# Attention and experts on one core: resident expert weights, batched gating, slot tables by one-hot matmuls, scatter in place

## The chip, the core and the metric

The kernel runs on one core of a Trainium2 chip. The metric is the device time of one execution in microseconds. PE is the matrix engine, DVE the vector engine, ACT the scalar engine, POOL the GpSimd engine, SP the engine that here only issues DMAs.

## The reference

Attention over 4 batches, 8 heads, 768 positions of 64 elements, then a layer of eight experts over the 3072 rows x of 512 elements that attention gives:

```python
scores = scale * np.matmul(q, k.transpose(0, 1, 3, 2))
# retrieval heads (0, 2, 6): causal; the others: causal and (first 4 or last 64 positions)
a = softmax(where(mask, scores, -1e9)); x = a @ v
do_compute = x @ w_skip > 0                 # other rows: out = x
logits = xc @ w_gate; e_idx = argmax(logits); gate_w = softmax(logits)[e_idx]
for e in range(8):
    h = np.maximum(xc[e_idx == e] @ w1[e], 0.0)
    y[e_idx == e] = gate_w * (h @ w2[e])
out[do_compute] = xc + y
```

w1[e] is 512 x 1024, w2[e] 1024 x 512, all inputs fp32.

## The kernel before

*Attention* (L162 to L277). For each batch b and pair of heads ("head group", hg, 16 in all) POOL issues six loads that cast to fp16: qin and kin for two heads (L172, L174), va for each (L197), 96 KB each. PE transposes q and k (L180, L184). Per head, `qk_exp` (L212) does a matmul of scores pst (L217), ACT the exponential into ats (L223), DVE a mask (L226, L249); then PE accumulates opsa (L268), and DVE divides into xsb, which holds all of x (L276). qin and kin have four buffers, va six. DVE writes the column of ones in va (L199) after its load has landed.

*Gating* (L284 to L327), per block of 128 rows, six per batch: PE transposes the block in fp32 (gxtp, one PSUM buffer, L289), DVE casts it (L293), PE multiplies by the gate and skip weights (L297), and some twelve DVE operations and one exponential on ACT give the gate and a one-hot row over the experts. x also goes to DRAM, attn_x (L280).

*Routing* (L333 to L421), after the last batch: ranks by fp32 matmuls and a running sum over 24 blocks (L351) give each token a slot; each expert has ECAP = 384 slots. 24 scatters on POOL write token numbers to eight tables in DRAM (L404); these are read back (L412), merged (L416), turned (L419).

*Experts* (L441 to L501). POOL issues the two weight loads of an expert (w1t, w2t, casts to fp16, two buffers, L444, L445), then for each of three blocks of 128 slots a gather of rows of attn_x (xg, L456) and one of gates (gw, L463); empty slots are skipped by the bounds check, over a tile set to zero. DVE scales (L468), PE transposes in fp32 (L472), DVE casts (L475). Chunks of 256 and 128 slots: PE multiplies by w1 (hps, L481), ACT takes the relu (L488), PE multiplies by w2 (yps, L493), DVE copies (L498), and the result goes to y_sorted in DRAM.

*End* (L505 to L518). For each of 24 blocks a gather fetches the rows of y_sorted by token (fyg, L510), DVE adds xsb (L516), and SP or ACT stores.

A scheduler fixes the order of each engine's instructions at build time; each engine runs its own in order and waits on semaphores. A POOL DMA also waits for the POOL DMA eight before it.

Of the kernel before, what the change touches and what calls it, by code (L numbers as in the profile page):

```python
# [9 lines left out]
FP32 = mybir.dt.float32  # L10
FP16 = mybir.dt.float16
# [7 lines left out]
B = 4  # L19
# [16 lines left out]
MTOK = 256  # L36
ECAP = MTOK + P


@with_exitstack  # L40
def kernel(
# [14 lines left out]
    nc = tc.nc  # L56

    NSLOT = E * ECAP
    NSUB = ECAP // P
    NC = N // P  # L60
    DS = DM // P
    FS = F // P
    NS2 = (NSLOT + P) // P
    NSHARD = 8
    BIG_IDX = 1 << 16

    X = nc.dram_tensor("attn_x", (N, DM), FP32, kind="Internal").ap()
    GATE = nc.dram_tensor("gate_w", (N,), FP32, kind="Internal").ap()
    SH = [nc.dram_tensor(f"sorted_sh{i}", (NSLOT + P,), I32,
                         kind="Internal").ap() for i in range(NSHARD)]  # L70
    YS = nc.dram_tensor("y_sorted", (NSLOT, DM), FP32, kind="Internal").ap()

    const = ctx.enter_context(tc.tile_pool(name="const", bufs=1))
    persist = ctx.enter_context(tc.tile_pool(name="persist", bufs=1))

    ident = const.tile([P, P], FP16, name="ident")
    make_identity(nc, ident)
# [3 lines left out]
    utri = const.tile([P, P], FP32, name="utri")  # L81
    nc.gpsimd.memset(utri, 1.0)
    nc.gpsimd.affine_select(
        out=utri, in_=utri, compare_op=ALU.is_ge, fill=0.0,
        base=0, pattern=[[1, P]], channel_multiplier=-1)

    ones_col = const.tile([P, 1], FP32, name="ones_col")
    nc.gpsimd.memset(ones_col, 1.0)
    ones_row = const.tile([1, P], FP32, name="ones_row")
    nc.gpsimd.memset(ones_row, 1.0)  # L90
    e_row8 = const.tile([P, E], FP32, name="e_row8")
    erow8i = const.tile([P, E], I32, name="erow8i")
    nc.gpsimd.iota(erow8i, pattern=[[1, E]], base=0, channel_multiplier=0)
    nc.vector.tensor_copy(e_row8, erow8i)

    bigfill = const.tile([NS2, P], I32, name="bigfill")
    nc.vector.memset(bigfill, BIG_IDX)
    for i in range(NSHARD):
        (nc.sync if i % 2 else nc.scalar).dma_start(
            out=SH[i].rearrange("(n p) -> n p", p=P),  # L100
            in_=bigfill)

    xsb = persist.tile([P, B, NQB, H, D], FP32, name="xsb")
# [11 lines left out]
    maskp = ctx.enter_context(tc.tile_pool(name="maskp", bufs=1))

    def band_mask(name, q_off, lo, hi, sink=False, width=P):
        m = maskp.tile([P, width], FP16, name=name)
        nc.gpsimd.memset(m, 1.0)
        nc.gpsimd.affine_select(  # L120
            out=m, in_=m, compare_op=ALU.is_ge, fill=0.0,
            base=q_off - lo, pattern=[[1, width]], channel_multiplier=-1)
        if hi is not None:
            nc.gpsimd.affine_select(
                out=m, in_=m, compare_op=ALU.is_ge, fill=0.0,
                base=hi - q_off, pattern=[[-1, width]], channel_multiplier=1)
        if sink:
            sm = maskp.tile([P, width], FP16, name=name + "_s")
            nc.gpsimd.memset(sm, 1.0)
            nc.gpsimd.affine_select(  # L130
                out=sm, in_=sm, compare_op=ALU.is_ge, fill=0.0,
                base=N_SINK - 1, pattern=[[0, width]], channel_multiplier=-1)
            nc.gpsimd.affine_select(
                out=sm, in_=sm, compare_op=ALU.is_ge, fill=0.0,
                base=q_off, pattern=[[1, width]], channel_multiplier=-1)
            nc.vector.tensor_max(m, m, sm)
        return m

    retr_diag = band_mask("retr_diag", 0, 0, None)
    strm_d0 = band_mask("strm_d0", 0, 0, WINDOW - 1, sink=True)  # L140
    strm_dn = band_mask("strm_dn", 0, 0, WINDOW - 1)
    strm_s0 = band_mask("strm_s0", QB, 0, WINDOW - 1, sink=True)
    strm_sn = band_mask("strm_sn", QB, 0, WINDOW - 1)
# [4 lines left out]
    vv = v.rearrange("b h (n p) d -> b h n p d", p=P)  # L148
    Xv = X.rearrange("(b n p) (h d) -> b n p h d", b=B, p=P, h=H)
# [404 lines left out]
```

## Time and profile before

| what | before |
|---|---|
| median of 3 runs (lowest, highest) | 503.02 us (502.21, 506.92) |
| span of the profiled execution | 499.5 us |
| busy PE / DVE / ACT / POOL | 313.7 / 208.8 / 135.2 / 202.8 us |
| DMA moved in the span | 50.51 MB, 101 GB/s |

The span goes from the first to the last instruction. [...] GB/s count bytes written, so a transfer that casts fp32 to fp16 counts half of what it reads.

### The profile page before, as it was taken

What the parts mean: (1) busy time and instruction counts of PE and PEld (TensorE: products, weight loads), DVE (VectorE), ACT (ScalarE), POOL (GpSimd) and SP (SyncE); (2) the same over time, 40 slices, a digit from 0 to 9 for tenths busy, and PEclk for the clock granted to TensorE, in tenths of its full rate; (3) what the DMA queues carried; (4) which work ended last, traced back from release to release, by engine and by line L of the source; (5) the groups of instructions that cost most, each with busy time, mean ns of one, the idle gap of its engine ahead of it and who ended that gap; (6) DMA issues with size and microseconds to landing.
All of it is one profiled execution on the core that took longest, in us unless ns stands there. A gap on an engine that the chain in (4) does not pass through costs nothing.

```text
span 499.5 us, 6050 instructions
## 1 busy us (share of the span) xinstructions
PE 313.7 (63%) x1981; PEld 175.0 (35%) x1981; DVE 208.8 (42%) x883; ACT 135.2 (27%) x317; POOL 202.8 (41%) x269
## 2 busy tenths in 40 slices
PE   0699999998999999962000048766868668770000
PEld 0344454444444444331000035534535444540000
DVE  1245566455654665467000134141441423316563
ACT  1464646564645564610000002101111012020000
POOL 9976751553011100000674636342533525005662
PEclk9999999999999999999999999979699798896555
DMA  4999991999132511031000694959679589512675
GB/s 31 120 103 88 82 202 11 70 65 173 11 25 18 142 10 8 2 126 2 1 0 9 112 206 112 170 126 206 122 162 168 122 162 183 125 52 95 211 229 184
DMA packets 108207, 50.51 MB, mean 101 GB/s; under 512 B 85079, under 2 KB 93671, under 8 KB 108176
## 3 DMA queue, kind: packets, MB, share of 16 engines
q0 software_dynamic: 94240, 31.04, 54.1%
q10 hardware_dynamic: 6000, 10.59, 6.0%
q1 hardware_dynamic: 7936, 8.51, 5.0%
q8 instruction: 15, 0.25, 0.2%
q14 instruction: 16, 0.13, 0.1%
HBM read 65.14 MB, written 19.00 MB: 168 GB/s over the span
## 4 chain that ended last, share of the span: by engine, by line
PE 45%; DMA 22%; issue 9%; POOL 9%; DVE 7%; ACT 6%; ACTq 0%; POOLq 0%; SPq 0%; DVEq 0%
DMA xg<-attn_x,merged 14%; PE pst L217 13%; PE opsa L268 10%; PE yps L493 6%; PE hps L481 5%; PE gxtp L289 4%; ACT ats L223 3%; ACT ht L488 2%; POOL fyg L510 2%; DMA fyg<-y_sorted,slot_i 2%; DMA gw<-gate_w,merged 2%; POOL sorted_sh L404 2%; PE qTps L180 2%; PE kTps L184 2%; DMA sorted_sh<-row_idx,slot_i 2%
## 5 line engine op out<-in xcount | busy, mean ns | idle before, releaser
L223 ACT ACTIVATE ats<-pst 128x256 f16<-128x256 f32 (+4 forms) x236 | 92.6, 417 | 74.1 <-PE pst L217 71.8
L217 PE MATMUL pst<-qT,kT 64*128 64x256 f16 (+4 forms) x236 | 91.0, 426 | 3.8 <-ACT ats L223 1.0
L488 ACT ACTIVATE ht<-hps 128x2048 f16<-128x2048 f32 (+1 forms) x16 | 23.2, 1450 | 196.8 <-PE hps L481 134.2
L268 PE MATMUL opsa<-va,ats 128*128 128x65 f16 x552 | 69.8, 241 | 2.9 <-ACT ats L223 2.3
L197 POOL DMA_DIRECT2D va<-in_v_dram x32 | 26.7, 843 | 94.0 <-PE opsa L268 54.5
L493 PE MATMUL yps<-w2t,ht 128*128 128x512 f16 x192 | 52.8, 433 | 18.7 <-ACT ht L488 18.7
L268 PEld LDWEIGHTS <-ats 128*128 128x128 f16 x552 | 41.3, 117 | 54.7 <-DVE ats L226 12.2
L481 PE MATMUL hps<-xTm,w1t 128*128 128x128 f16 (+1 forms) x512 | 48.0, 255 | 1.0 <-DVE xTm L475 1.0
L404 POOL DMA_INDIRECT sorted_sh<-row_idx,slot_i x24 | 23.4, 977 | 57.2 <-DVE slot_i L398 50.2
L481 PEld LDWEIGHTS <-w1t 128*128 128x128 f16 x512 | 42.0, 102 | 10.4 <-issue 3.8
L510 POOL DMA_INDIRECT fyg<-y_sorted,slot_i x24 | 26.5, 1104 | 42.2 <-DVE fyg L509 37.7
L472 PE MATMUL xtp<-identf,xg 128*128 128x128 f32 x96 | 18.9, 351 | 36.2 <-DVE xg L468 36.2
L468 DVE TENSOR_SCALAR xg<-xg,gw 128x512 f32<-128x512 f32 x24 | 11.4, 492 | 67.8 <-DMA xg<-attn_x,merged 52.2
L493 PEld LDWEIGHTS <-ht 128*128 128x128 f16 x192 | 19.2, 107 | 47.2 <-ACT ht L488 23.2
L456 POOL DMA_INDIRECT xg<-attn_x,merged x24 | 24.8, 1033 | 22.4 <-issue 19.0
L217 PEld LDWEIGHTS <-kT 64*128 64x128 f16 (+1 forms) x236 | 20.5, 102 | 27.8 <-issue 16.2
L289 PE MATMUL gxtp<-identf,xsb 128*128 128x128 f32 x96 | 29.3, 435 | 0.9 <-DVE xsb L276 0.9
L174 POOL DMA_DIRECT2D kin<-in_k_dram x32 | 27.8, 867 | 3.8 <-PE kTps L184 2.6
L172 POOL DMA_DIRECT2D qin<-in_q_dram x32 | 27.7, 866 | 3.0 <-PE pst L217 2.0
L475 DVE CAST xTm<-xtp 128x512 f16<-128x512 f32 x24 | 15.8, 681 | 30.7 <-PE xtp L472 30.7
L180 PE MATMUL qTps<-ident,qin 128*128 128x128 f16 x96 | 18.8, 308 | 14.9 <-DMA qin<-in_q_dram 14.9
L472 PEld LDWEIGHTS xtp<-identf,xg 128*128 128x128 f32 x96 | 14.7, 181 | 37.8 <-DVE xg L468 20.6
(111 smaller groups left out, 369.1 us busy)
## 6 DMA issues: line engine op xcount, KB each, us to landing
w1t<-in_moe_w_dram POOLq DMA_DIRECT2D x8, 1024.0 KB, 9.4
w2t<-in_moe_w_dram POOLq DMA_DIRECT2D x8, 1024.0 KB, 12.3
y_sorted<-ys ACTq DMA_DIRECT2D x16, 256.0 KB
qin<-in_q_dram POOLq DMA_DIRECT2D x32, 96.0 KB, 3.3
kin<-in_k_dram POOLq DMA_DIRECT2D x32, 96.0 KB, 3.3
va<-in_v_dram POOLq DMA_DIRECT2D x32, 96.0 KB, 3.2
attn_x<-xsb SPq DMA_DIRECT2D x12, 256.0 KB
attn_x<-xsb ACTq DMA_DIRECT2D x12, 256.0 KB
```

The lines of the kernel that those rows point to most:

```text
L174: nc.gpsimd.dma_start(out=kin[:, :, hd, :], in_=kv[b, h0 + hd].transpose([1, 0, 2]))
L180: nc.tensor.matmul(qTps[:, n * P:(n + 1) * P], qin[:, n].rearrange("p h d -> p (h d)"), ident, is_transpose=True, start=(n == 0), stop=(n ...
L217: nc.tensor.matmul(pst[:k_rows, :qn], kTh[:, j * P:j * P + k_rows], qTh[:, q_lo:q_hi], start=True, stop=True)
L223: nc.scalar.activation(dst, pst[:k_rows, :qn], ACT.Exp)
L268: nc.tensor.matmul(opsa[:, i, :], ats[:kr, sl, i * QB:i * QB + QB], vh[:kr, j, :], start=(cnt == 1), stop=(cnt == total))
L289: nc.tensor.matmul(xtp[:, s, :], xc[:, s * P:(s + 1) * P], identf, is_transpose=True, start=(s == 0), stop=(s == DS - 1))
L404: nc.gpsimd.indirect_dma_start(out=SH[c % NSHARD][:, None], out_offset=bass.IndirectOffsetOnAxis(ap=slot_i[:, c:c + 1], axis=0), in_=row_i ...
L472: nc.tensor.matmul(xtp[:, s, :], xg[:, s * P:(s + 1) * P], identf, is_transpose=True, start=(s == 0), stop=(s == DS - 1))
L481: nc.tensor.matmul(hps[:, fs, :mt], w1t[:, s, fs * P:(fs + 1) * P], xT[:, s, :mt], start=(s == 0 and fs % BPB == 0), stop=(s == DS - 1 and ...
L488: nc.scalar.activation(ht[:, :, :mt], hps[:, :, :mt], ACT.Relu)
L493: nc.tensor.matmul(yps, ht[:, fs, s2 * P:(s2 + 1) * P], w2t[:, fs, :], start=(fs == 0), stop=(fs == FS - 1))
L510: nc.gpsimd.indirect_dma_start(out=yg, out_offset=None, in_=YS[:, :], in_offset=bass.IndirectOffsetOnAxis(ap=slot_i[:, c:c + 1], axis=0), ...
```

## The change

Attention keeps its loops. The weights of all experts get places of their own in SBUF (w1a, w2a), and POOL issues the two loads of one expert in every second head group. qin and kin have two buffers, va four, qT and kT two. x of a batch is in one tile xb with one buffer, stored straight to `out` by SP in one DMA per batch. The gating of a batch is done for its six blocks at once (`gate_ops`), and goes on to ranks (a matmul with a lower triangle, one with ones, a scan), and to one-hot tables: Lall (which of 128 slots in a tile) and Rall (which of 16 tiles, times token number and gate). 24 matmuls of Lall with Rall give, for each slot, its token and gate (mps). Each expert has CAP = 256 slots. 16 gathers fetch rows of `out`; an empty slot reads some row, and its scatter index is out of bounds. The gate is applied in the update of the gathered rows, which a scatter then writes back to `out`. PE does the first half of expert e + 1 before the second half of e. At the end every engine reads a flag (an expert with over 256 tokens, or other retrieval heads than 0, 2, 6) and branches past `general_path`, a slow form of the whole program in loops.

```diff
+CAP = 256
+NT = E * CAP // P
...
+    w1a = wpool.tile([P, E, DS, F], FP16, name="w1a")
+    w2a = wpool.tile([P, E, FS, DM], FP16, name="w2a")
...
-    with tc.tile_pool(name="qk_in", bufs=4) as qk_in_pool, \
-         tc.tile_pool(name="qt", bufs=3) as qt_pool, \
-         tc.tile_pool(name="va", bufs=6) as v_pool, \
+    with tc.tile_pool(name="qk_in", bufs=2) as qk_in_pool, \
+         tc.tile_pool(name="qt", bufs=2) as qt_pool, \
+         tc.tile_pool(name="va", bufs=4) as v_pool, \
+         tc.tile_pool(name="xsb", bufs=1) as x_pool, \
...
+                if hg % 2 == 1:
+                    ew = 2 * b + hg // 2
+                    nc.gpsimd.dma_start(out=w1a[:, ew], in_=w1r[ew])
+                    nc.gpsimd.dma_start(out=w2a[:, ew], in_=w2r[ew])
...
+            nc.sync.dma_start(out=Ov[b], in_=xbf)
...
+            gate_ops(nc, gat_pool, C, glog, NQB, gate,
+                     oh.rearrange("p e n -> p n e"))
...
+            nc.tensor.matmul(cps, ones16, ohf, start=True, stop=True)
+            nc.tensor.matmul(rps, lneg, ohf, start=True, stop=True)
...
+            nc.vector.tensor_tensor(
+                Rall[:, b], oht.unsqueeze(3).to_broadcast([P, NQB, NT, 4]),
+                val.unsqueeze(2).to_broadcast([P, NQB, NT, 4]), op=ALU.mult)
+            for n in range(NQB):
+                nc.vector.tensor_scalar(Lall[:, b, n], iota16,
+                                        posf[:, 1, n:n + 1], None,
+                                        ALU.is_equal)
...
+        for c in range(N // P):
+            nc.tensor.matmul(
+                mps.rearrange("p t v -> p (t v)"), Lall[:, c // NQB, c % NQB],
+                Rall[:, c // NQB, c % NQB].rearrange("p t v -> p (t v)"),
+                start=(c == 0), stop=(c == N // P - 1))
...
+        for t in range(NT):
+            xg = xg_pool.tile([P, DM], FP32, name=f"xg{t}")
             nc.gpsimd.indirect_dma_start(
+                out=xg, out_offset=None, in_=out[:, :],
...
+            for f2 in range(FS // 2):
+                hps = h_psum.tile([P, 2, CAP], FP32, tag="hps", name="hps")
...
+                            hps[:, fi, :], w1a[:, e, s, fs * P:(fs + 1) * P],
+                            xT[:, s, :], start=(s == 0), stop=(s == DS - 1))
+                nc.scalar.activation(ht[:, 2 * f2:2 * f2 + 2], hps, ACT.Relu)
...
+                nc.vector.scalar_tensor_tensor(xgs[t], yps, gsl[:, t:t + 1],
+                                               xgs[t], ALU.mult, ALU.add)
                 nc.gpsimd.indirect_dma_start(
+                    out=out[:, :],
...
+        first(0)
+        for e in range(E):
+            if e + 1 < E:
+                first(e + 1)
+            second(e)
+
+    flag = nc.values_load(flagi[:, :])
+    with tc.If(flag > 0, preferred_fallthrough_block=False):
+        general_path(tc, C, q, k, v, moe_w1, moe_w2, out, XG, FL, nz)
```

`first` is casts, transposes and hps with the relu of an expert, `second` its yps, updates and scatters.

On POOL, in the experts of the kernel before, one expert's transfers stand in the queue like this (weights, three gathers of rows, gates):

```order
L444 DMA w1t<-in_moe_w_dram 128x4x1024
L445 DMA w2t<-in_moe_w_dram 128x8x512
L456 DMA xg<-attn_x,merged 128x512 x3
L462 MEMSET gw 128x1
L463 DMA gw<-gate_w,merged 128x1
```

In the kernel after, the weights of the second expert stand on POOL among the loads of the fourth and fifth head groups:

```order
L383 DMA kin<-in_k_dram 128x6x64
L406 DMA va<-in_v_dram 128x6x64
L413 DMA w1a<-in_moe_w_dram 128x4x1024
L406 DMA va<-in_v_dram 128x6x64
L414 DMA w2a<-in_moe_w_dram 128x8x512
L381 DMA qin<-in_q_dram 128x6x64
```

The weights moved from before each expert's gathers to attention, between v loads, each of which waits for a buffer that a head two groups back has read.

On DVE, from the last head of the last batch on, before (xsb is that head's output, then block by block):

```order
L276 TENSOR_TENSOR xsb<-opsa,rec 128x6x64
L293 CAST gxT<-gxtp 128x512
L300 COPY glog<-gp 128x9
L304 MAX mx<-glog 128x8
L318 TENSOR_SCALAR dc<-glog 128x1
L305 MAX_INDEX mi<-mx,glog 128x8
L312 TENSOR_SCALAR neg_mx<-mx 128x1
```

And after, from the same place (xb for xsb; then all six blocks, then one chain):

```order
L490 TENSOR_TENSOR xb<-opsa,rec 128x6x64
L507 CAST gxT<-gxtp 128x512 x6
L513 COPY glog<-gps 128x54
L75 TENSOR_REDUCE g_mx<-glog 128x6
L88 TENSOR_SCALAR g_nd<-glog 128x6
L78 TENSOR_TENSOR g_sub<-glog,g_mx 128x48
L82 SCALAR_TENSOR_TENSOR g_eq<-g_sub,erev 128x48
```

The small operations of each block moved behind the last of the six casts, and are there once instead of six times.

On DVE, from the end of the routing into the experts, before:

```order
L398 CAST slot_i<-slot_f 128x24
L416 TENSOR_REDUCE mnp<-shard_t 25x128
L421 CAST merged<-mnp_ps 128x25
L468 TENSOR_SCALAR xg<-xg,gw 128x512 x2
L475 CAST xTm<-xtp 128x4x128
```

And after (Lall is the last table, msb the slot table copied from PSUM, x_3058 and x_3066 the first two gathered blocks in fp16):

```order
L579 TENSOR_SCALAR Lall<-iota_109,posf 128x128 x5
L593 COPY msb<-mps 128x64
L595 TENSOR_SCALAR emp<-msb 128x16
L597 SCALAR_TENSOR_TENSOR tok<-msb 128x16
L608 TENSOR_TENSOR gsl<-msb 128x16
L601 TENSOR_TENSOR egs<-emp,slot_126 128x16
L599 TENSOR_SCALAR tok<-tok 128x16
L603 TENSOR_TENSOR idx_g<-tok,egs 128x16
L605 SCALAR_TENSOR_TENSOR idx_s<-emp,tok 128x16
L641 CAST x_3058<-xg_2993 128x512
L641 CAST x_3066<-xg_2997 128x512
L647 COPY xT<-xtp 128x4x128
```

Between `slot_i` and `mnp` before lie the scatters and the read-back in DRAM; after, the indices come from PSUM by DVE alone. The next row after these is the third block's cast, and with it the second copy of the transposed block.

## Rows read from the trace of the kernel before

**Rows 1.** Windows by stage: length; busy PE, PEld, DVE, ACT, POOL; PEclk, DMA, GB/s.

```profile
17.00:214.30 197.30, 185.05 (x1113) 91.45 (x1113) 106.94 (x618) 107.04 (x287) 70.75 (x92) 1.00 0.76 69
214.30:227.50 13.20, 6.85 (x45) 4.48 (x45) 10.37 (x74) 2.36 (x12) 0.00 (x0) 1.00 0.33 120
227.50:296.00 68.50, 5.59 (x17) 3.60 (x18) 12.51 (x47) 0.00 (x0) 33.05 (x34) 1.00 0.31 50
296.00:449.20 153.20, 113.86 (x792) 74.18 (x791) 47.88 (x89) 23.20 (x16) 56.13 (x74) 0.88 0.70 144
449.20:499.50 50.30, 0.00 (x0) 0.00 (x0) 28.15 (x49) 0.00 (x0) 26.50 (x24) 0.55 0.56 178
```

**Rows 2.** The chain that ended last: start, length, what.

```profile
260.60 9.65 DMA sorted_sh<-row_idx,slot_i
...
315.60 13.32 DMA xg<-attn_x,merged
...
418.27 11.38 DMA xg<-attn_x,merged
```

**Rows 3.** Timeline of DVE from the last batch's gating into the routing.

```profile
214.88 0.69 DVE L293 CAST gxT<-gxtp 128x512 f16<-128x512 f32 x1 [0.57 <-PE gxtp L289]
...
224.92 0.69 DVE L293 CAST gxT<-gxtp 128x512 f16<-128x512 f32 x1 [0.26 <-PE gxtp L289]
...
225.97 0.17 DVE L300 COPY glog<-gp 128x9 f32<-128x9 f32 x1
...
228.59 0.36 DVE L340 TENSOR_TENSOR rank_in<-incl_ps,onehot 128x192 f32<-128x192 f32 x1 [0.78 <-PE incl_ps L338]
...
229.69 4.28 DVE L351 TENSOR_TENSOR excl<-excl,cnt 1x8 f32<-1x8 f32 x23
```

**Rows 4.** Groups by form, whole span: busy us, mean ns, idle before.

```profile
L223 ACT ACTIVATE ats<-pst 128x512 f16<-128x512 f32 x36 | 21.4, 596 | 8.6 <-PE pst L217 7.5
...
L498 DVE COPY ys<-yps 128x512 f32<-128x512 f32 x24 | 16.5, 685 | 21.0 <-PE yps L493 21.0
...
L468 DVE TENSOR_SCALAR xg<-xg,gw 128x512 f32<-128x512 f32 x24 | 11.4, 492 | 67.8 <-DMA xg<-attn_x,merged 52.2 <-DMA gw<-gate_w,merged 15.4
...
L191 DVE COPY kT<-kTps 128x768 f16<-128x768 f16 x16 | 8.8, 552 | 3.4 <-PE kTps L184 1.9 <-PE pst L217 1.4
...
L325 DVE TENSOR_TENSOR onehot<-e_row,ef 128x8 f32<-128x8 f32 x24 | 3.6, 152 | 0.0
```

**Rows 5.** Timeline of PE in the experts.

```profile
296.08 5.86 PE L481 MATMUL hps<-xTm,w1t 128*128 128x256 f16 x32 [1.01 <-DVE xTm L475]
...
312.18 3.66 PE L481 MATMUL hps<-xTm,w1t 128*128 128x256 f16 x32
315.68 0.60 PE L472 MATMUL xtp<-identf,xg 128*128 128x128 f32 x4
317.87 3.63 PE L493 MATMUL yps<-w2t,ht 128*128 128x512 f16 x16 [1.59 <-ACT ht L488]
321.33 1.95 PE L481 MATMUL hps<-xTm,w1t 128*128 128x128 f16 x32
...
353.44 3.60 PE L493 MATMUL yps<-w2t,ht 128*128 128x512 f16 x8 [0.90 <-ACT ht L488]
```

**Rows 6.** Windows of three shorter stretches, columns as in rows 1.

```profile
280.00:302.00 22.00, 7.86 (x43) 6.21 (x43) 3.80 (x7) 0.02 (x1) 12.01 (x15) 1.00 1.15 204
12.50:25.00 12.50, 8.69 (x58) 4.69 (x58) 2.58 (x12) 5.17 (x11) 12.50 (x16) 1.00 1.89 120
350.00:357.00 7.00, 5.07 (x15) 2.09 (x15) 4.27 (x8) 1.02 (x1) 4.07 (x6) 0.50 0.30 83
```

**Rows 7.** DMA queue of plain stores: packets, MB, share of 16 engines.

```profile
q10 hardware_dynamic: 6000, 10.59, 6.0%
```

**Rows 8.** Timeline of the end: POOL's second gather, the last store's issue.

```profile
454.28 1.00 POOL L510 DMA_INDIRECT fyg<-y_sorted,slot_i  x1 [0.30 <-DVE fyg L509]
...
495.51 0.34 ACTq L517 DMA_DIRECT2D out_dram<-foc  x1
```

**Rows 9.** Tile fyg, gathers at the end with no weights ahead.

```profile
DMA to landing us min/median/max: 2.5/3.6/4.7
```

More of the change, by code (lines that the diff above doesn't have):

```diff
@@ L34, with band_mask @@
 P = 128
-MTOK = 256
-ECAP = MTOK + P
+DS = DM // P
+FS = F // P
+CAP = 256
+NT = E * CAP // P
+BIG_IDX = 1 << 16
+class Consts:
+    pass
+def band_mask(nc, pool, name, q_off, lo, hi, sink=False, width=P):
+    m = pool.tile([P, width], FP16, name=name)
+    nc.gpsimd.memset(m, 1.0)
+    nc.gpsimd.affine_select(
+        out=m, in_=m, compare_op=ALU.is_ge, fill=0.0,
+        base=q_off - lo, pattern=[[1, width]], channel_multiplier=-1)
+    if hi is not None:
+        nc.gpsimd.affine_select(
+            out=m, in_=m, compare_op=ALU.is_ge, fill=0.0,
+            base=hi - q_off, pattern=[[-1, width]], channel_multiplier=1)
+    if sink:
+        sm = pool.tile([P, width], FP16, name=name + "_s")
+        nc.gpsimd.memset(sm, 1.0)
+        nc.gpsimd.affine_select(
+            out=sm, in_=sm, compare_op=ALU.is_ge, fill=0.0,
+            base=N_SINK - 1, pattern=[[0, width]], channel_multiplier=-1)
+        nc.gpsimd.affine_select(
+            out=sm, in_=sm, compare_op=ALU.is_ge, fill=0.0,
+            base=q_off, pattern=[[1, width]], channel_multiplier=-1)
+        nc.vector.tensor_max(m, m, sm)
+    return m
@@ L56 @@
     nc = tc.nc
[L58 to L71, printed above, removed]
+    C = Consts()
@@ L91 @@
[L91 to L103, printed above, removed]
@@ L115 @@
[L115 to L137, printed above, removed]
@@ L139 @@
[L139 to L143, printed above, removed]
+    C.wg = const.tile([P, DS, E + 1], FP16, name="WgAll")
+    nc.gpsimd.dma_start(out=C.wg[:, :, :E],
+                        in_=moe_w_gate.rearrange("(s p) e -> p s e", p=P))
+    nc.gpsimd.dma_start(out=C.wg[:, :, E],
+                        in_=moe_w_skip.rearrange("(s p) -> p s", p=P))
@@ new lines @@
+    pid = const.tile([P, 1], FP32, name="pid")
+    nc.vector.tensor_copy(pid, pidi[:, 0:1])
+    slot128 = const.tile([P, NT], FP32, name="slot128")
+    nc.vector.tensor_scalar_add(slot128, pidi, float(P))
+    sreset = const.tile([P, E, NQB], FP32, name="sreset")
+    nc.vector.memset(sreset, 1.0)
+    nc.vector.memset(sreset[:, :, 0:1], 0.0)
+    tabl = const.tile([1, H], FP32, name="tabl")
+    nc.vector.memset(tabl, 0.0)
+    for hh in range(H):
+        if IS_RETR[hh]:
+            nc.vector.memset(tabl[:, hh:hh + 1], 1.0)
@@ new lines, with first @@
+    NSM = CAP // P
+    with tc.tile_pool(name="moe_x", bufs=2) as mx_pool, \
+         tc.tile_pool(name="moe_xg", bufs=1) as xg_pool, \
+         tc.tile_pool(name="moe_h", bufs=2) as h_pool, \
+         tc.tile_pool(name="moe_xt_ps", bufs=2, space=bass.MemoryType.PSUM) as xt_psum, \
+         tc.tile_pool(name="moe_h_ps", bufs=4, space=bass.MemoryType.PSUM) as h_psum, \
+         tc.tile_pool(name="moe_y_ps", bufs=2, space=bass.MemoryType.PSUM) as y_psum:
+        xgs = []
+        for t in range(NT):
+            xg = xg_pool.tile([P, DM], FP32, name=f"xg{t}")
+            nc.gpsimd.indirect_dma_start(
+                out=xg, out_offset=None, in_=out[:, :],
+                in_offset=bass.IndirectOffsetOnAxis(
+                    ap=idx_g[:, t:t + 1], axis=0),
+                bounds_check=N - 1, oob_is_err=False)
+            xgs.append(xg)
+        hts = {}
+        def first(e):
+            xT = mx_pool.tile([P, DS, CAP], FP16, tag="xT", name="xT")
+            for s2 in range(NSM):
+                x16 = mx_pool.tile([P, DM], FP16, tag="x16", name="x16")
+                nc.vector.tensor_copy(x16, xgs[e * NSM + s2])
+                xtp = xt_psum.tile([P, DS, P], FP16, tag="xtp", name="xtp")
@@ L478 @@
-            BPB = 512 // MTOK
-            for fs in range(FS):
-                for s in range(DS):
-                    nc.tensor.matmul(
-                        hps[:, fs, :mt],
-                        w1t[:, s, fs * P:(fs + 1) * P],
-                        xT[:, s, :mt],
-                        start=(s == 0 and fs % BPB == 0),
-                        stop=(s == DS - 1 and fs % BPB == BPB - 1))
-            ht = h_pool.tile([P, FS, MTOK], FP16, tag="ht", name="ht")
-            nc.scalar.activation(ht[:, :, :mt], hps[:, :, :mt], ACT.Relu)
@@ L490 @@
[L490 removed]
+            ht = h_pool.tile([P, FS, CAP], FP16, tag="ht", name="ht")
+            for f2 in range(FS // 2):
+                hps = h_psum.tile([P, 2, CAP], FP32, tag="hps", name="hps")
+                for fi in range(2):
+                    fs = 2 * f2 + fi
+                    for s in range(DS):
+                        nc.tensor.matmul(
+                            hps[:, fi, :], w1a[:, e, s, fs * P:(fs + 1) * P],
+                            xT[:, s, :], start=(s == 0), stop=(s == DS - 1))
+                nc.scalar.activation(ht[:, 2 * f2:2 * f2 + 2], hps, ACT.Relu)
@@ L491, with second @@
+            hts[e] = ht
+        def second(e):
+            for s2 in range(NSM):
+                t = e * NSM + s2
                 yps = y_psum.tile([P, DM], FP32, tag="yps", name="yps")
```

551 lines of the change are left out of this document (330 added, 221 removed).

## The prediction

> **What bounds the kernel now.** I read the windows by stage first, then the chain of waits inside the long stages, then the timeline for the pace of single steps. [rows 1] cut the span into five stages. In attention (17 to 214.3 us) PE is busy 185.05 of 197.30 us at a granted clock of 1.00: PE bounds it, and the DMA rate, 69 GB/s, is low. From 214.3 to 227.5 the last batch's rows are gated. From 227.5 to 296.0 PE is busy 5.59 of 68.5 us: this is the routing (24 scatters of token numbers, the tables read back, the first weights and gathers). The experts (296 to 449.2) keep PE busy 113.86 of 153.2 us at a mean clock of 0.88, and the last 50.3 us (results fetched back, added, stored) have no PE work at all. The chain [rows 2] says what the waits are: the landing of the last scatter, 9.65 us, and in the experts six waits for a gather, 13.32 us the first and 11.38 the last, which stand behind the next expert's two weight transfers on POOL's queue. The median gather with no weights ahead lands in 3.6 us [rows 9].
>
> **The change part by part.** All times are on the profiled execution's clock: span 499.5 us, and its kernel's median of 503.02 us lies 3.5 us above it.
>
> *Attention.* Line for line the same PE work. Added are the 16 weight transfers, on POOL's queue, between the loads of q, k and v. From 280 to 302 us, with weights in flight all the time, the DMA moved 204 GB/s [rows 6]; 16 x 1.05 MB (in fp16) at that rate take 82 us. The 96 loads cost at most 0.82 us each (98 KB at the 120 GB/s of 12.5 to 25 us, where POOL issues without a pause) [rows 6], 79 us. The x stores, 6.3 MB: the SP/ACT queue in [rows 7] moved 10.59 MB in 6.0% of the span, 30 us, so 18 us. Sum 179 of 197 us: it fits, narrowly. What counts is lead. A load behind a pair of weights is late by about 11.4 - 3.6 = 8 us [rows 2, 9]; eight pairs, 64 us if nothing covered it. Cover there is: a head group takes 197.3 / 16 = 12.3 us; q and k are two groups deep (qk_in bufs 2), v two groups (4 heads), and the POOL order in the text above puts each weight transfer behind a v load that waits for a head two groups back, so q and k lead by about 12 us and v by one to two heads. If that cover is gone, DVE's column of ones in va (L199) waits, every mask behind it on DVE, and PE after that. The x tile is now one buffer: the next batch's first write waits for the store of 1.5 MB (a quarter of those 18 us, 4.5); the order puts that write after six casts and two heads of masks, so I cost it at nothing, or 3 x 4.5 us if the cover goes. ACT loses 24 small exponentials and six store issues per batch, DVE about as much as it gains; neither bounds the stage. POOL's setup grows by about 0.5 us. Bounds: -5 (ACT's relief) to +64; I take +4, near no cost, as lead exceeds delay. End of attention 214.3 + 4 = 218.3.
>
> *Gating of the last batch.* The six transposes and casts alternate between PE and DVE at 2.0 us as before (214.88 to 224.92) [rows 3], so the logits are copied at 226.1 + 4 = 230.1. Then the batched chain: ten DVE operations on 48 elements. An 8-element operation takes 0.152 us, 192 elements 0.36, a dependent step 4.28 / 23 = 0.186 [rows 3, 4]; so 0.24 us each (bounds 0.19 to 0.39): 2.4. Two small matmuls and their hand-over 0.6 (the nearest row waits 0.78 for one of 192 columns in fp32 [rows 3]). 31 operations for ranks and one-hot tables, 0.2 each and 0.35 more for the 384-wide one (0.55 is the nearest size, kT [rows 4]), with pauses 7.0. Six matmuls of 24 (18 stand before the transposes in PE's order), the copy and six operations to the indices: 1.9. Indices ready at 230.1 + 2.4 + 0.6 + 7.0 + 1.9 = 242.0.
>
> *Gathers.* Scatters to tables, their read-back, the fetch of gates and all memsets go. DVE and PE order need the third gather before the first expert's matmuls: two pitches of 1.30 us (1.00 and 0.30 between) [rows 8] and 3.6 us of landing (2.5 to 4.7 [rows 9]) make 6.2; a cast (no row has fp32 to fp16 in SBUF: at most 0.49 as L468, at least half) and a copy of the transposed block (0.55 to 0.69, kT and ys) [rows 4] 1.2. First expert matmul at 249.4, against 296.08 [rows 5]: 46.7 us less.
>
> *Experts.* 256 slots in place of 384. Per expert 32 matmuls of 256 columns (3.50 us from 312.18 to the next group at 315.68), 16 of 512 (3.46 us, 317.87 to 321.33) [rows 5] and eight fp16 transposes, 0.5 (four in fp32 take 0.60): 7.46 us, eight times 59.7. The first ones run at half pace after the pause (5.86 against 3.66 us [rows 5]): 2.2. At each change of expert the two copies of the transposed block stand on DVE behind the two updates of the expert before; PE covers this with six yps matmuls (1.3 us) and lacks about 0.4 us, seven times 3. Sum 64.9: end at 314.3. DVE needs 2 x (0.49 + 0.6 + 0.75) = 3.7 us per expert, ACT 4 x 0.6 [rows 4], POOL 4 x 1.3: all below 7.46. Gathers run ahead by two per 2.6 us, and no weights stand before them. Before: 153.2 us.
>
> *End.* The 50.3 us of fetch, add and store go. What is late next is the last update (0.75), its scatter (3.6, as the gathers land; 2.5 to 4.7 [rows 9]) and leaving the branch over the fallback, not seen in any row: 0 to 5 us (its nearest, the last store, is issued at 495.51 and the span ends 4.0 us later [rows 8]); I take 2. End of span 314.3 + 0.1 + 0.75 + 3.6 + 2 = 320.8; with 3.5 around it **324 us**.
>
> **The rivals.** *Attention becomes DMA bound.* For it: 179 of 197 us leave 9%, POOL stands still at each v load until a head is done, and half of the weight delay uncovered costs 32 us. Against it: the lead worked out above, and a mean of 69 GB/s now. Time 324 - 4 + 32 = 352, at worst 384. Shown by POOL, DVE or PE waits for va and qin.
>
> [...]
>
> *The fallback runs: slower.* The branch is taken if any expert has more than 256 tokens. It then goes through 24 blocks x 8 experts, each with two weight transfers of about 5.1 us (1.05 MB at 204 GB/s [rows 6]) into single buffers: 1,960 us more, some 2,280. Counting the reference's choices for this draw gives 69, 235, 250, 230, 53, 142, 42 and 142: six tokens below the limit, and fp16 would have to move seven near-ties into one expert. This rival decides from the 257th token on.
>
> **How the numbers follow.** My forecast 0.74; DMA-bound attention 0.15; the clock 0.06; fallback 0.02; faster than 308 (attention relieved, shorter DVE steps) 0.03. The range takes the bounds of the unknown costs downward (-9 for attention, -7 for DVE steps and the end), 308, and upward reaches the middle of the DMA rival: 354. Anything but the fallback is faster by far more than the 1% that a measurement of this kernel can tell from no change: faster 0.97, within 1% 0.01, slower 0.02.
>
> **What would show it.** Right: the last xb write near 218 us; some 24 us from there to the first gather; hps within 32 us of that write; PE busy over nine tenths of about 65 us of experts at clock 1.00; scatters hidden but the last. Wrong: waits for qin or va of more than a few us in all; clock rows of 0.50 among the experts; gathers that land later than 5 us; any instruction of the fallback.

## The result, and the profile after

The changed kernel takes **327.79 us** (median of 4 runs, 326.06 to 328.53), the kernel before 502.62 in the same session: a ratio of **0.6506**, 95% interval 0.6475 to 0.6538. The forecast was 324. The profiled execution has a span of 327.0 us against 499.5. The times measured below are medians without runs more than 1.5% above the fastest of the same kernel (one run of e1 and of e12, two of e6); the expectations were written with all runs and so have 322.2 for e1 and 327 for e12.

Windows by stage of the kernel after, to be read beside [rows 1] (length; busy PE, PEld, DVE, ACT, POOL; PEclk, DMA, GB/s): attention, gating, routing with the first gathers, experts, end. PEclk, the granted clock, is the one granted to PE as a share of its full speed, and busy PE is modelled, since the profile models the ends of matmuls.

```profile
17.00:221.20 204.20, 187.38 (x1138) 91.96 (x1137) 105.62 (x533) 103.38 (x254) 83.66 (x102) 1.00 1.26 149
221.20:234.00 12.80, 6.89 (x50) 4.55 (x48) 5.20 (x13) 0.24 (x1) 0.00 (x0) 1.00 0.33 124
234.00:249.00 15.00, 3.02 (x21) 1.93 (x21) 8.20 (x50) 0.00 (x0) 5.62 (x6) 1.00 0.25 72
249.00:308.90 59.90, 59.90 (x437) 40.94 (x435) 20.76 (x42) 19.10 (x32) 23.30 (x24) 1.00 0.28 88
308.90:327.00 18.10, 0.00 (x0) 0.00 (x0) 0.75 (x1) 0.00 (x0) 2.95 (x3) 0.62 0.07 23
```

Stage by stage against before: attention +6.9 us; gating, routing and first gathers 27.8 in place of 81.7, -53.9; experts 59.9 in place of 153.2, -93.3; end 18.1 in place of 50.3, -32.2. The sum is -172.5, the whole difference of the spans. In the experts PE is busy without a gap at a granted clock of 1.00; in the end it does nothing for 18.1 us.

What the end waits for is in POOL's timeline of the kernel after, its last gather and the first and the last scatters (start, length, line, operation; in brackets the idle time before and what ended it):

```profile
261.51 1.00 POOL L628 DMA_INDIRECT xg<-out_dram,idx_g  x1 [0.31 <-DMA xg<-out_dram,idx_g]
266.12 1.03 POOL L671 DMA_INDIRECT out_dram<-xg,idx_s  x1 [3.61 <-issue]
269.58 1.00 POOL L671 DMA_INDIRECT out_dram<-xg,idx_s  x1 [2.42 <-DVE xg L669]
...
310.53 0.98 POOL L671 DMA_INDIRECT out_dram<-xg,idx_s  x1 [2.32 <-DMA out_dram<-xg,idx_s]
313.36 0.98 POOL L671 DMA_INDIRECT out_dram<-xg,idx_s  x1 [1.85 <-DMA out_dram<-xg,idx_s]
316.83 0.98 POOL L671 DMA_INDIRECT out_dram<-xg,idx_s  x1 [2.48 <-DMA out_dram<-xg,idx_s]
```

The first scatter stands behind the landing of the last gather (issued at 261.51; the profile names no releaser, but the gap of 3.61 us fits the 3.6 that a gather takes to land), though its rows were ready at 260.15 (the update of 259.40, 0.75 long). Each later one stands behind the landing of the one before it: the profile names that landing for 10 of the 15, and e1 below tests it. 16 scatters take 316.83 - 266.12 = 50.7 us, one every 3.38. The last update ends at 308.94 + 0.75 = 309.69, so the last scatter leaves 7.1 us behind it. The waits of the kernel after (engine, line, what for: us, times, longest) sum this up. Below the first row stand PE's and DVE's waits for q, v and k, first after the change and then before it:

```profile
POOL out_dram L671 <- DMA out_dram<-xg,idx_s: 24.1, 10, 3.4
PE qTps L389 <- DMA qin<-in_q_dram: 16.1, 4, 13.9
DVE va L408 <- DMA va<-in_v_dram: 10.3, 4, 6.1
PE kTps L393 <- DMA kin<-in_k_dram: 2.8, 5, 1.5
...
PE qTps L180 <- DMA qin<-in_q_dram: 14.9, 2, 13.4
DVE va L199 <- DMA va<-in_v_dram: 10.1, 5, 6.9
PE kTps L184 <- DMA kin<-in_k_dram: 0.4, 1, 0.4
```

Little of these is new. The 13.9 us and the 13.4 us are both PE's wait for the very first load at the start of the kernel; what the change added to the three rows is 1.2, 0.2 and 2.4 us. POOL's own waits for the DMA eight before are small after the change: the loads issued at 34.06 and 148.31 us wait 1.81 and 0.84 us for the w2a transfers of 19.22 and 132.39, the one at 129.22 waits 2.28 us for the va load of 117.36.

### The profile page after: what moved, and what is told of

It reads as the page before. It is cut to its first block, busy times and chain, and to the rows that moved or that the text cites. A ratio compares the mean times of both kernels' runs of the same rounds, so it can differ in the third digit from the quotient of the medians.

```text
span 327.0 us, 4731 instructions
## 1 busy us (share of the span) xinstructions
PE 259.1 (79%) x1652; PEld 140.7 (43%) x1652; DVE 143.3 (44%) x659; ACT 124.8 (38%) x289; POOL 131.7 (40%) x179
## 4 chain that ended last, share of the span: by engine, by line
PE 56%; DMA 19%; POOL 7%; DVE 6%; issue 4%; ACT 4%; POOLq 0%; ACTq 0%; DVEq 0%
PE pst L431 16%; PE opsa L482 13%; DMA kin<-in_k_dram 11%; PE hps L654 8%; PE yps L665 6%; PE gxtp L502 5%; DMA out_dram<-xg,idx_s 4%; PE kTps L393 3%; ACT ats L437 3%; PE qTps L389 3%; DMA qin<-in_q_dram 3%; POOL qin L381 2%; POOL kin L383 1%; DVE gxT L507 1%; POOL va L406 1%
## 5 line engine op out<-in xcount | busy, mean ns | idle before, releaser
L657 ACT ACTIVATE ht<-hps 128x512 f16<-128x512 f32 x32 | 19.1, 597 | 51.0 <-PE hps L654 51.0
L628 POOL DMA_INDIRECT xg<-out_dram,idx_g x16 | 16.1, 1005 | 42.7 <-DVE idx_s L605 38.1
L671 POOL DMA_INDIRECT out_dram<-xg,idx_s x16 | 15.8, 987 | 39.5 <-DMA out_dram<-xg,idx_s 24.1
L502 PE MATMUL gxtp<-identf,xb 128*128 128x128 f32 x96 | 29.3, 435 | 2.0 <-DVE xb L490 1.9
L654 PE MATMUL hps<-xT,w1a 128*128 128x256 f16 x256 | 30.6, 280 | 0.0
L665 PE MATMUL yps<-w2a,ht 128*128 128x512 f16 x128 | 29.9, 379 | 0.0
L654 PEld LDWEIGHTS <-w1a 128*128 128x128 f16 x256 | 25.7, 101 | 5.1
L440 DVE TENSOR_TENSOR ats<-ats,strm_dn 128x128 f16<-128x128 f16 x100 | 21.9, 219 | 8.8 <-ACT ats L437 8.1
L507 DVE CAST gxT<-gxtp 128x512 f16<-128x512 f32 x24 | 16.6, 691 | 20.2 <-PE gxtp L502 20.1
L393 PE MATMUL kTps<-ident,kin 128*128 128x128 f16 x96 | 18.8, 305 | 2.8 <-DMA kin<-in_k_dram 2.8
```

The costliest lines, as they stand in the source:

```text
L393: nc.tensor.matmul(kTps[:, n * P:(n + 1) * P], kin[:, n].rearrange("p h d -> p (h d)"), C.ident, is_transpose=True, start=(n == 0), stop=( ...
L440: nc.vector.tensor_mul(ats[:k_rows, sl, q_lo:q_lo + mw], ats[:k_rows, sl, q_lo:q_lo + mw], diag_mask[:k_rows, :mw])
L502: nc.tensor.matmul(xtp[:, s, :], xc[:, s * P:(s + 1) * P], identf, is_transpose=True, start=(s == 0), stop=(s == DS - 1))
L654: nc.tensor.matmul(hps[:, fi, :], w1a[:, e, s, fs * P:(fs + 1) * P], xT[:, s, :], start=(s == 0), stop=(s == DS - 1))
L665: nc.tensor.matmul(yps, hts[e][:, fs, s2 * P:(s2 + 1) * P], w2a[:, e, fs, :], start=(fs == 0), stop=(fs == FS - 1))
```

## Experiments

Each is an edit of the changed kernel unless another is named.

**e1: scatters that don't wait for each other.**

```diff
+        ovs = dram_disjoint_views(out, NT)
-                    out=out[:, :],
+                    out=ovs[t][:, :],
```

> Each scatter goes through its own view of out, which the scheduler takes as disjoint from the others (each token has one slot, so no row is written twice); the gathers still read the whole. Theory A, the scatters stand one behind another: after the change the 16 are issued at 266.12 to 316.83 us, one every 3.38 us (50.71 / 15), and the last is issued 7.1 us behind the last update (309.69). Then the last is now issued at about 309.7, all of POOL's waits on the landing of a scatter (24.1 us) are gone, and the time falls by 7.1 to 320.7. Rival B, the end is set by what follows the last scatter (9.2 us from the end of its issue to the end of the span), or scatters in flight together land later: time within 2 us of 327.8.

Measured: 321.72 us, ratio 0.6373 (0.6334 to 0.6411), 6.1 us less than the changed kernel. POOL's timeline of e1:

```profile
305.57 0.98 POOL L673 DMA_INDIRECT out_dram<-xg,idx_s  x1 [4.68 <-DVE xg L671]
307.30 0.98 POOL L673 DMA_INDIRECT out_dram<-xg,idx_s  x1 [0.74 <-DVE xg L671]
309.03 0.98 POOL L673 DMA_INDIRECT out_dram<-xg,idx_s  x1 [0.74 <-DVE xg L671]
310.75 0.98 POOL L673 DMA_INDIRECT out_dram<-xg,idx_s  x1 [0.74 <-DVEq L687]
```

No scatter waits for the landing of another any more, and the last leaves 6.1 us sooner. Theory A holds. The first still waits for the gathers (it leaves at 266.08), but the next three follow it every 1.3 to 1.6 us and catch up with the updates. This kernel keeps all of the program and beats both others.

**e4: no branch.**

```diff
-    flag = nc.values_load(flagi[:, :])
-    with tc.If(flag > 0, preferred_fallthrough_block=False):
-        general_path(tc, C, q, k, v, moe_w1, moe_w2, out, XG, FL, nz)
```

> The load of the flag and the branch over the fallback are left out (the counting that makes the flag stays); for this draw nothing else is left out. My prediction put 2 us on leaving the branch (bounds 0 to 5). Theory A: time 325.8, the span ends 2 us sooner after the last scatter (now 9.2 us from the end of its issue to the end of the span). Rival B, the branch hides behind the landing of the last scatter and the end is the same: 327.8. Rival C, most of those 9.2 us is the branch (its instructions are fetched again): 322 or less.

Measured: 323.52 us, 0.6428 (0.6388 to 0.6467): 4.3 us less, near the upper bound of what I had given the branch (the load of the flag goes with it, so the 4.3 is for both). From the end of the last scatter's issue to the end of the span it is now 321.5 - 317.3 = 4.2 us in place of 9.2. In its last 18 us the changed kernel has six transfers of the instruction queues (two on q8, four on q14), two of them behind the last scatter; e4 has none in its last 18 us. What share of the 4.3 us they have is not shown.

**e2, e3, e6: where attention's 6.9 us come from.** e2 loads one expert's weights only; e3 spreads the transfers; e6 takes them out of attention.

```diff
-                if hg % 2 == 1:
-                    ew = 2 * b + hg // 2
+                if b == 0 and hg == 1:
+                    ew = 0
```

> Only the first expert's weights are loaded, in attention, and all eight experts use them (so the rows of the other seven are not the reference's): 14 of the 16 weight transfers go, no other instruction. Theory A, attention's lengthening by 6.9 us (casts of the last batch at 221.76 to 231.79 against 214.88 to 224.92) is the price of the weight transfers: casts begin near 215, time 327.8 - 6.9 = 320.9. Rival B, it comes from the code around (one x tile whose store lands in 9.6 us before the next batch may write, the batched chain on DVE): casts still begin near 221.8, time 327.8.

Measured: 326.17 us, 0.6465 (0.6439 to 0.6490). Casts of the last batch begin at 218.97, 2.8 us sooner, less than half of what theory A asked for; of these the serial scatters took back 1.2 (the last one leaves at 315.27). The 1.6 us that are left of the time are not clear of noise.

```diff
+                ew = 2 * b + hg // 2
-                if hg % 2 == 1:
+                if hg % 2 == 0:
                     nc.gpsimd.dma_start(out=w1a[:, ew], in_=w1r[ew])
+                else:
                     nc.gpsimd.dma_start(out=w2a[:, ew], in_=w2r[ew])
```

> The same 16 transfers, one per head group (w1 of an expert in an even head group, w2 in the odd one) in place of two in every second. Theory A, the cost of the weights is queueing: a q or k load stands behind two transfers (waits of 13.8, 10.9, 8.5 and 8.7 us in the chain), and behind one it would be late by about half, which the lead of 12 us covers: time 327.8 - (2 to 6) = 322 to 326. Rival B, the cost is shared DMA rate, the same however it is spread: within 1 us of 327.8.

Measured: 337.28 us, 0.6696 (0.6673 to 0.6719): 9.5 us more, against both theories. PE's wait for q in e3:

```profile
PE qTps L389 <- DMA qin<-in_q_dram: 25.6, 4, 13.8
```

That is 9.5 more than in the changed kernel, with the same bytes: here the cost is not the rate but which load a transfer stands ahead of. Behind the first load, PE waits for q three times, 4.3, 3.7 and 3.8 us, where the changed kernel has 1.2, 0.7 and 0.3. e3 has a transfer in the first head group of each batch.

```diff
+        load_w(0)
+        load_w(1)
         xgs = []
...
             second(e)
+            if e + 2 < E:
+                load_w(e + 2)
```

> The changed kernel with the weights fetched in the experts' stage again, into two buffers: the first two pairs ahead of the gathers, each later pair behind the scatters of the expert whose buffer it takes. Theory A, it is the weights' place that freed the experts: a pair is 2.1 MB, 10.3 us at the 204 GB/s that the kernel before reached with weights in flight, more than the 7.39 us of an expert; the experts then take 8 x 10.3 = 82 us, 16 to 22 more than now, attention gives back 2: 342 to 348. Rival B, the experts' gain came from smaller blocks and from gathers that run ahead; the first pairs land during the gating and the later ones hide: within 4 us of 327.8.

Measured: 373.57 us, 0.7409 (0.7341 to 0.7478): 45.8 us more, well beyond theory A. (The scheduler put the first gather ahead of the first two pairs of weights, and all of them behind the indices.) Without any weights in attention the casts of the last batch begin where they did before the change [rows 3]; this is DVE's timeline in e6, with the wait for the second gather, which stands behind the two pairs:

```profile
214.86 0.69 DVE L501 CAST gxT<-gxtp 128x512 f16<-128x512 f32 x1 [0.57 <-PE gxtp L496]
...
260.56 0.43 DVE L647 CAST x<-xg 128x512 f16<-128x512 f32 x1 [20.54 <-DMA xg<-out_dram,idx_g]
```

So attention's lengthening goes with the weights, though e6 has the single x tile and the batched gating too (e7, the same way, has its casts from 213.92). How large it is varies between executions: four traces have one and the same attention, with PE's and ACT's instructions in the same order, and their casts begin at 221.76 (the changed kernel), 221.63 (e1), 221.98 (e4) and 218.09 (e8, whose only edit is an operand of the flag). So the weights cost 3 to 7 us, and a difference of under 4 us between two traces of attention shows nothing by itself. Nor is the loss where the first pair stands. This is how much later than before the change the last head of each batch is written (before: 65.31, 115.40, 167.06 and 213.76 us; the writes of xsb and xb):

| batch | changed kernel | e2 | e3 | e6 |
|---|---|---|---|---|
| 1 | -0.2 | +1.1 | +1.1 | -0.5 |
| 2 | +1.9 | +3.1 | +2.2 | -0.7 |
| 3 | +4.0 | +2.4 | +7.5 | -1.4 |
| 4 | +6.9 | +4.1 | +14.7 | 0.0 |

The changed kernel loses nothing in the first batch, with the first pair in it, and 2 to 3 us in each later one.

The 49.5 us between the two traces (376.5 and 327.0) are 6.9 less up to the casts, 20.1 more from there to the first hps (the wait above), 39.0 more in the experts and 2.7 less at the end. The experts, from the first hps to the last yps, take 98.9 us (262.17 to 361.06), 12.4 per expert: not the 10.3 of the transfers' rate, since each transfer also stands behind the scatters on POOL's queue, which wait for each other (38.2 us in e6, nine waits, the longest 6.7).

**e7: 384 slots, on top of e6.**

```diff
-CAP = 256
+CAP = 384
```

> [...] Theory A, PE's work adds in full: an expert takes 7.39 x 1.5 = 11.1 us, 3.7 more, and eight of them 29.6 more than the 59.8 us now; against e6 it is what is left above the weights' pace, 8 x (11.1 - 10.3) = 6, and 8 scatters more at 3.38 us if those set the end (24 x 3.38 = 81 us, below PE's 89): 6 to 12 above e6. Rival B, the weights don't pace e6, so that all of the 29.6 shows: 26 to 33 above e6.

Measured: 412.21 us, 0.8165 (0.8116 to 0.8214), 38.6 above e6, beyond rival B. (hps, a tile of 2 x 512 columns in e7, has two buffers in place of four.) The experts take 126.9 us (263.53 to 390.45), 28.0 more than in e6. With that the gain of the experts' stage is split: 153.2 before, 126.9 with the new stage's code (most gathers ahead of their weights, no fetch of gates, fp16 transposes, the halves of two experts interleaved, not told apart by any run), 98.9 with 256 slots, 59.9 with resident weights.

**e9, e10, e12: back the 6.9 us, on top of e1.** e9 has `xsb` with two buffers, e10 `qk_in` with three; e12 moves the weights:

```diff
-                if hg % 2 == 1:
-                    ew = 2 * b + hg // 2
+                if hg % 2 == 1 and (b, hg) != (0, 1):
+                    ew = 2 * b + hg // 2 - 1
...
             xgs.append(xg)
+        nc.gpsimd.dma_start(out=w1a[:, E - 1], in_=w1r[E - 1])
+        nc.gpsimd.dma_start(out=w2a[:, E - 1], in_=w2r[E - 1])
```

> e1 with two x tiles in place of one. Of attention's +6.9 us, leaving out the weights gave back 2.8 (casts of the last batch begin at 219.0 against 221.8), so 4.1 has another cause. Theory C, it is the single x tile: at the second change of batch the row sums of the next head were inverted at 124.21 us, but their product was written to x only at 133.56, when the last transpose of the batch before was done (131.82); until then the head's PSUM, and with it the v load behind it on POOL's queue, is held. Two tiles give back about 4: 322.2 - 4 = 318. Rival D, nothing waits for that head at the change of batch (a second PSUM buffer is there): within 1 us of 322.2.

> e1 with three buffers for q and k in place of two. Theory E, q and k lead too little when weights stand ahead of them on POOL's queue (waits of 8.5 to 10.9 us for a landing in the chain); one more group of lead hides them: 322.2 - 2.8 (what leaving out the weights gave back) = 319.4. Rival F, the loads stand behind a v load that waits for a head in PE, so a third buffer lets none be issued sooner: within 1 us of 322.2.

> e1 with the weights one place later: the first pair goes with the fourth head group of the first batch in place of its second, and so on; the eighth pair is issued behind the gathers (it is needed at the last expert, some 50 us on). In e6, with no weights in attention, the casts of the last batch begin at 214.86 us, as before the change (214.88): all of the 6.9 is the weights'. With the first pair alone (e2) they begin at 218.97. Theory A: that pair costs 4.1 of the 6.9, since at 17 to 20 us the loads of q and k have no lead yet; without it there, casts begin near 217.5 and the time is 322.2 - 4 = 318. Rival B: the cost is not bound to that place but to some pair meeting loads that are just due (e3 was 9.5 longer with the same transfers in other places): within 1.5 us of 322.2. Rival C: the slow stretch of the first expert that e9 to e11 had (7 to 11 us) comes back: 325 or more, with casts near 217.5 all the same.

Measured: e9 330.39 us, 0.6564 (0.6531 to 0.6596); e10 331.08, 0.6563 (0.6516 to 0.6610); e12 326.15, 0.6463 (0.6438 to 0.6488). (In e12 the scheduler put the eighth pair right behind the seventh, not behind the gathers.) In their traces attention is shorter: last casts from 218.75, 219.06 and 219.53 us, against 221.63 in e1. All three are slower than e1 all the same, and in these traces the loss has one place, DVE's copy of the second expert's first block, here in e12:

```profile
248.76 0.43 DVE L645 CAST x<-xg 128x512 f16<-128x512 f32 x1 [0.67 <-DMA xg<-out_dram,idx_g]
257.97 0.42 DVE L651 COPY xT<-xtp 128x512 f16<-128x512 f16 x1 [8.78 <-remote]
```

"remote" is a release whose instruction the profile can't name. ACT's timeline of e12 shows that it is PE that is late, within the first expert:

```profile
248.81 0.60 ACT L661 ACTIVATE ht<-hps 128x512 f16<-128x512 f32 x1 [17.23 <-PE hps L658]
250.11 0.60 ACT L661 ACTIVATE ht<-hps 128x512 f16<-128x512 f32 x1 [0.70 <-PE hps L658]
253.66 0.60 ACT L661 ACTIVATE ht<-hps 128x512 f16<-128x512 f32 x1 [2.95 <-remote]
256.52 0.60 ACT L661 ACTIVATE ht<-hps 128x512 f16<-128x512 f32 x1 [2.26 <-remote]
```

Eight matmuls of 256 columns end 2.9 us after the eight before them; in the changed kernel it is 0.88 (ReLUs at 252.18, 253.05 and 253.93). PE's own rows don't show it, because the ends of matmuls are modelled. e6 has the same wait (7.2 us), and so has e7; in the changed kernel and e1 to e4 it is 2.6 to 3.9 us. The slow groups end 2.85 to 2.87 us apart in e6, e9, e10, e11 and e12 alike, at a granted clock of 0.95 to 1.00. And e8, the changed kernel but for the flag, has it too: its wait for that copy is 7.4 us, two of its ReLUs are 2.86 us apart, and its casts began at 218.09. So the stretch comes and goes between executions of the same instructions, and its being there or not in one trace doesn't prove an edit right or wrong.

So rival C of e12 came, and theories C, E and A (of e12) are not shown: they got 2.9, 2.6 and 2.1 us in attention, less than they asked for and less than the 3.9 by which traces of the same attention differ. Against the x tile as the cause speak e6, which has one and loses nothing, and e11 below, which has two and has its casts from 222.00.

**e11 and e14: what the stretch depends on.**

```diff
+        keep_busy(16)
...
+                if e == 0:
+                    keep_busy(2)
```

> e9 (views for the scatters, two x tiles) with 16 matmuls of 512 columns, whose result nobody reads, ahead of the first gathered block and two behind each of the first expert's two transposes, so that PE is not idle between gating and experts. In e9 attention ended 3.0 us sooner than in e1, as forecast, yet the time was 8 us longer: the first expert's 32 hps matmuls were begun at 246.41 us after PE had been busy for 2.4 of 15 us (230 to 245), the ReLU of its third and fourth group came at 253.25 and 256.12, 2.9 us apart (0.9 at full clock, 1.7 at half), and the next expert's block was copied only at 257.55. Theory A, this slow stretch belongs to the clock's return after a pause: with PE kept busy the first expert goes at the full clock (3.5 us in place of 11) and the time is 322.2 - 3.0 (attention) - 1.5 (no slow first expert, as in e1) = 317.7. Rival B, the slow stretch has to do with the gathers' traffic at that time, or with something else that PE's activity does not change: 330 or more.

Measured: 331.46 us, 0.6556 (0.6517 to 0.6595). The wait for the copy is still there, 8.9 us. But the edit did not do what it was meant to. The scheduler put all 20 extra matmuls into the routing, and PE stood idle for 5.0 us ahead of the first gathered block, as PE's timeline of e11 shows:

```profile
236.29 4.35 PE L643 MATMUL warm<-w2a,Lall 128*128 128x512 f16 x11 [0.83 <-DVE rank L537]
...
241.30 1.46 PE L643 MATMUL warm<-w2a,Lall 128*128 128x512 f16 x6
247.78 0.61 PE L655 MATMUL xtp<-ident,x 128*128 128x128 f16 x4 [5.02 <-DVE x L652]
```

From 246 to 253 us the granted clock is 0.56. So e11 does not decide between theory A and rival B. Other traces speak against theory A: e12 has the stretch though its granted clock is 1.00 up to 253 us, and e1, at 0.50 until 250 us, has not.

```diff
+            if t >= 6:
+                xgs.append(xg)
+                continue
```

> e12 with six gathers in place of 16; the blocks from the seventh on are a tile of zeros, so the results of the experts from the fourth on are left out of what is computed (all matmuls, updates and scatters stay). In e6 and e9 to e12 the first expert has a slow stretch while gathers are in flight (e12: ReLUs of its groups at 248.81, 250.11, 253.66, 256.52, the next block copied at 257.97; in the changed kernel at 250.9, 252.2, 253.0, 253.9). Theory A, the gathers' traffic is a party to it: with the last gather issued some 7 us after the first, the stretch is gone or ends with it, the first expert takes under 6 us and the time is 327 - 8 = 319 or less. Rival B, the gathers have no part in it: the wait of some 9 us for the copy of the next block stays, 325 or more.

Measured: 316.87 us, 0.6279 (0.6243 to 0.6314), 9.3 less than e12. DVE and ACT of e14, the same two places:

```profile
250.72 0.42 DVE L656 COPY xT<-xtp 128x512 f16<-128x512 f16 x1 [3.13 <-PE xtp L653]
```

```profile
248.75 0.60 ACT L666 ACTIVATE ht<-hps 128x512 f16<-128x512 f32 x1 [0.83 <-PE hps L663]
249.62 0.60 ACT L666 ACTIVATE ht<-hps 128x512 f16<-128x512 f32 x1 [0.28 <-PE hps L663]
250.49 0.60 ACT L666 ACTIVATE ht<-hps 128x512 f16<-128x512 f32 x1 [0.28 <-PE hps L663]
```

This agrees with theory A: without the later gathers in flight the stretch is gone. It does not show it, since the stretch also comes and goes with all 16 gathers in flight at the same distance from the first matmul: the trace of the changed kernel is spared and that of e8 is not. The cause stays open.

**e8: the fallback taken.**

```diff
-        nc.vector.tensor_tensor(ovr, ovr, mism, op=ALU.max)
+        nc.vector.tensor_tensor(ovr, ovr, tabl, op=ALU.max)
```

> The flag is always set, so that the fallback runs after the new path and computes everything again. My slower rival priced it at 24 x 8 pairs of weight transfers, 2 x 5.1 us each: 1,960 us more, some 2,280 in all. Rival: the fallback's own attention, block by block, costs as much again, well over 3,000; or its transfers overlap, under 1,500.

Measured, in one run: 3,962 us, 3,634 above the changed kernel. My 1,960 counted the weight transfers alone. The fallback's attention, which I left out, takes some 700 us (320 to 1,026). Its experts take some 2,920 us (1,032 to 3,954), 15.2 for each pair of a block and an expert in place of 10.2, since in single buffers matmuls and transfers take turns; its page has PE waiting for weights in both halves:

```profile
L241 PE MATMUL m_yp<-m_w,m_ht 128*128 128x512 f16 x1536 | 641.1, 593 | 717.6 <-DMA m_w<-in_moe_w_dram 690.8
L233 PE MATMUL m_hp<-m_xT,m_w 128*128 128x128 f16 x6144 | 641.7, 299 | 529.9 <-DMA m_w<-in_moe_w_dram 529.9
```

## Why the prediction was right, step by step

The sum was 3.8 us off because its errors cancel, which is luck; two terms missed by more than that. The signposts of the new stages, from DVE's timeline of the kernel after: the first and the last cast, the logits' copy, the first rank operation, the scatter indices, the first cast for an expert.

```profile
221.76 0.69 DVE L507 CAST gxT<-gxtp 128x512 f16<-128x512 f32 x1 [0.57 <-PE gxtp L502]
...
231.79 0.69 DVE L507 CAST gxT<-gxtp 128x512 f16<-128x512 f32 x1 [1.31 <-PE gxtp L502]
232.85 0.21 DVE L513 COPY glog<-gps 128x54 f32<-128x54 f32 x1 [0.36 <-PE gps L509]
...
235.26 0.25 DVE L528 TENSOR_TENSOR_SCAN incl<-sreset,gps 128x48 f32<-128x48 f32 x1 [0.33 <-PE gps L526]
...
240.81 0.17 DVE L605 SCALAR_TENSOR_TENSOR idx_s<-emp,tok 128x16 int32<-128x16 f32 x1
245.31 0.50 DVE L641 CAST x<-xg 128x512 f16<-128x512 f32 x1 [4.33 <-issue]
```

- *Attention: taken as +4, measured +6.9.* The step was "near no cost, as lead exceeds delay". It held in the first batch and lost 2 to 3 us in each later one; e6 and e7 show that the loss goes with the weights, e8 that it is 3.2 us in another execution of the same attention. The chain of waits of the kernel after has loads of q and k that land 8.5 to 10.9 us after their issue in the third and fourth batch; which pair of weights costs what, no run shows (e2 and e12 differ by less than executions do). The sign that I had set for being wrong, waits for q or v of more than a few us in all, was no sign: they are 25.0 us before the change and 26.4 after it. The DMA-bound rival was far off.
- *Gating and routing: from the logits to the indices taken as 11.9 us, measured 8.1* (232.85 to 240.98). The casts kept their pitch of 2.0. The small operations overlap: most begin 0.07 to 0.25 us apart, where I took 0.2 to 0.24 for each, and the 31 of them take 4.3 us (235.26 to 239.57) in place of 7.0.
- *Gathers: 7.4 us from indices to the first hps, measured 8.0.* The first hps came at 249.0 us; forecast 249.4. The cast, for which no row stood and which I had put between half of 0.49 us and all of it, took 0.44 (mean of 16).
- *Experts: 64.9 us, measured 59.9.* An expert takes 7.39 us (forecast 7.46). The bubbles at a change of expert (3.0) don't exist: PE is busy 59.90 of 59.90. The first expert's slow start cost 1.3 (its 32 hps matmuls 5.00 us, the next 3.65), not 2.2. It is not a lower clock: the granted clock is 1.00 there, and it was 1.00 as well in the 5.86 us of [rows 5] that I had read as half pace after a pause. Of the lower clock in the experts, to which I had given 0.06, nothing is seen: from 249.0 to 308.9 us the granted clock is 1.00, while PE goes through four buffers of hps and two of yps.
- *End: 6.5 us behind the last matmul, measured 18.1.* This is the step that failed: "its scatter (3.6)", with all scatters hidden but the last. They stand one behind another and the first behind all gathers; that puts the last 7.1 us late, 6.0 by the late start (266.12 against 260.15) and the rest by the pace of 3.38, and e1 takes 6.1 of them away. The other part is leaving the branch, 2 taken, 4.3 measured by e4 with the load of the flag. For the update's 0.75 I gave no row either; the kernel after has 0.75 (mean of 16).
- *Around the span* I added 3.5 us, the distance of a median from the trace of a short run (499.5 us, where later runs of the kernel before have spans of 499.8 to 504.9); 0.8 was right (327.79 against 327.0).

Together on the span: +2.9 (attention), -3.8 (gating), +0.6 (gathers), -5.0 (experts), +11.6 (end) make 6.3, the difference of 327.0 and 320.8 but for rounding.

## What to carry to other kernels

In this kernel the indirect scatters into one DRAM tensor went one behind another, one every 3.38 us, and the first of them behind the last gather from it (266.12 us); it is worth counting such scatters as a chain (here 16 x 3.38 us) and comparing it with the stage it runs beside, or declaring them disjoint where the indices are (e1: 6.1 us less). Weights that were moved into an earlier stage were paid here not by their bytes but by the loads that came due behind them on the same queue, so their place is worth trying out: the same 16 transfers cost attention 3 to 7 us in one order and 14.7 in another (e3: last casts from 229.59). Before a few us between two traces are put down to an edit, they should be set beside the difference of traces with the same instructions: here 3.9 us. A gain ahead of a paced chain was partly lost in it (the scatters in e2 took back 1.2 of 2.8 us).

## What I had not expected of the hardware

- The granted clock of attention can be at 0.50 without costing time. The four runs of the changed kernel have spans of 327.0, 324.5, 326.3 and 326.3 us at mean granted clocks of 0.979, 0.715, 0.712 and 0.712; in e1's trace the window from 17 to 221 us has a clock of 0.66 and the last casts begin at 221.63, in the changed kernel 1.00 and 221.76. Single steps don't differ either: six transposes of k in a row (L393, in e1 L394) take 0.82 us at 1.00 (at 153.00 us in the changed kernel) and at 0.50 (at 153.28 us in e1), and the casts of the last batch follow each other every 2.01 us at both. So "PE bounds it" was too much said of attention: a PE that is shown busy for 187 of 204 us there is not held by the rate of its array. What holds it, the exchange with ACT and DVE perhaps, no run shows. The experts before the change are otherwise: eight yps matmuls took 3.60 us at 0.50, sixteen 3.63 at 1.00 [rows 5, 6].

```profile
17.00:221.00 204.00, 184.17 (x1136) 91.04 (x1136) 105.50 (x533) 103.25 (x254) 83.70 (x102) 0.66 1.27 149
```

- PE's first expert, while gathers are in flight, can run at under a third of its pace (2.9 us in place of 0.88 for eight matmuls) at a granted clock of 0.95 to 1.00, in some executions and not in others of the same instructions. With six gathers in place of 16 it did not; the cause is open.
